# Operand sums of the seven-product stages placed anew, with the scale chain in two parts

## The chip, the cores and the metric

The kernel runs on one core of a Trainium2 chip. Its time is the device time of one execution in microseconds (us). The engines are named as in the profile: PE (TensorE, matmuls), PEld (its weight loads), DVE (VectorE), ACT (ScalarE), POOL (GpSimd) and SP (the engine that only issues DMAs). Each runs its own list of instructions in order, and waits on semaphores for the others.

## The reference

One transformer layer over x of 2048 x 1024. An attention part with 32 heads in four segments of 512 tokens, with a running memory matrix, makes `h = x + attention(layernorm(x)) @ wo`. A gated part follows:

```python
z  = gelu(layernorm(h) @ w_in)            # 2048 x 3584
z1 = z[:, :1792]
z2 = layernorm(z[:, 1792:])
g  = w_sp @ z2 + b_sp[:, None]            # w_sp is 2048 x 2048
h2 = h + (z1 * g) @ w_out                 # w_out is 1792 x 1024
```

The change touches the gated part alone.

## The kernel before

The attention part, which fills most of the first 340 us, is left as it is. Then these stages follow, and PE runs them in this order without a pause that is planned.

**The z2 half.** `z2_group(k, tc)` multiplies 128 tokens (tc, 16 of them) with 448 of the 1792 columns (k, 4 of them) in 8 matmuls; ACT applies the gelu, DVE takes the batch statistics (`z2_stats`), and with k = 3 also their aggregate, from which POOL makes the reciprocal deviation in two small instructions (tile `zrs`). Work for later stages is put between these groups: the list `aux`, filled by `at(q, f, ...)`, holds what is issued after group number q, where q is 16k + tc - 20. It holds the norms of `w_sp` and `w_in` for the scales, the half-precision copies of the z1 weights (`wz_half`), the first operand sums of the next stage (`hn_sum(0, ...)` on DVE, `sz_sum(0, ...)` on POOL).

**The z1 half.** z1 is made transposed. Blocks of 2 x 2 are multiplied with seven products in place of eight (Strassen's way in Winograd's form), which needs sums and differences of the operand blocks: `hn_sum(p, t, h)` for the activations (four sums t in two halves h, for each of the two token halves p) and `sz_sum(g, k)` for the weights (four for each of 14 steps g). `z1_step(g, k)` is product k of step g; the table `offs` orders the products, so that in steady state PE runs per step: 6 and 5, then 1 of the next step, 7, 2, 3 of the step before, and 4. Each is four matmuls of 512 columns. POOL makes the sums for step g + 1 when products 5 and 7 of step g are issued. What DVE and ACT do beside it is put into `todo1` by `on(g, k, f, ...)`, and is issued after product k of step g: the layer norm of z2 (`z2_apply`, after products 6 and 4), the second half's activation sums, the scale of `w_sp` (`scale_of`), its half-precision blocks (`sp_part`) and their sums (`sp_sum`).

**The gate, twice.** `gate(pr, ...)` multiplies half of `w_sp` with z2, again in seven products (b11, b12, b22, b21 and the sums t1 to t4), for seven column groups g. A product is `prod`: eight matmuls into one PSUM bank. Per group PE runs t2, t1, b11 of a later group (`p1`), t3, b21 of the next (`p2`), t4, b22. DVE takes the results from PSUM (`stt`), multiplies with z1 (`out`) and makes the sums of the z2 blocks (`ss`); POOL adds the bias (`tmp_s1b`), twice per group. The product t3 goes into the bank of t2, so it waits until DVE has read that bank.

**The output units between the gates.** 16 units of 14 matmuls each finish 1024 of the tokens. Each loads its piece of h (`fin_load`), adds on DVE, and stores. Both DMAs are issued by ACT, in ACT's program order: the load of unit n + 2, the store of unit n, and then, for n from 1 to 8, the square sum of an eighth of `w_out` (`wo_norm(n - 1)`, a 1792-element activation). In the same stretch SP loads the second half of `w_sp` by 16 transposing DMAs and, behind them in its queue, the two rows of biases (`brow_load(1)`); DVE converts and sums the blocks (`sp_half`, `sp_sum`). Two chains of scales run there. `scale_y` needs the square sums of the biases (`brow_sq`, on ACT) and of z1; it goes PE (`total`), DVE, POOL (four small instructions, the last a power), DVE, and scales the biases on ACT. `scale_w` needs the eight square sums of `w_out`, which POOL copies to `SQB`; a matmul (`total(8)`) sums them over the partitions. That matmul stands in PE's list after unit 11.

**The last stage.** The other 1024 tokens are multiplied with `w_out` in seven products too. Its weights and sums are made during the second gate (`ob_scale` on ACT, `ob_sum` on DVE, from the table in `each1`), its operand sums by `y_sum`. The last seventh of each sum (chunk 6) needs the gate's last result. `o_adds` makes three sums of a product and the residual on POOL; they are the operands of DVE's `o_stt`.

What orders each engine's work is thus the order in which the program issues it; no planner moves anything. Line numbers in the profile are all those of the recorder (L210), so groups are told by their tiles.

Of the kernel before, what the change touches and what calls it, by code (L numbers as in the profile page):

```python
# [10 lines left out]
ALU = mybir.AluOpType  # L11
# [247 lines left out]
def bass_sequential_preLN__memory_aug_infini_attn__mixer_gmlp__prompt_kernel(  # L259
# [17 lines left out]
    pe, act, dve, pool, sp = R.pe, R.act, R.dve, R.pool, R.sp  # L277
# [661 lines left out]
    def scale_of(k, n, b):  # L939
        b = next_bank() if b is None else b  # L940
        pe.matmul(PS[:, b, 0:n], ONES[:], SQB[:, 0:n], start=True, stop=True)
        dve.tensor_reduce(out=TOT[:], in_=PS[:, b, 0:n], axis=mybir.AxisListType.X, op=ALU.add)
        dve.tensor_single_scalar(TOT[:], TOT[:], 1e-30, ALU.max)
        if k:
            dve.reciprocal(TOP[:], TOT[:])
        else:
            pool.tensor_tensor(TOP[:], TOT[:], MHZ[:], ALU.pow)
        dve.tensor_single_scalar(TOP[:].bitcast(I32), TOP[:].bitcast(I32), 0x7F800000, ALU.bitwise_and)
        dve.tensor_single_scalar(SC[k][:], TOP[:], 8192.0, ALU.mult)
        dve.reciprocal(INV[k][:], SC[k][:])  # L950
# [40 lines left out]
    def at(q, f, *a):  # L991
        aux.setdefault(q, []).append((f, a))
# [12 lines left out]
    at(19, wz_norm, 3, 1)  # L1005
    at(20, pool.tensor_copy, SQB[:, 0:14], SQZ[:])
    at(25, scale_of, 1, 14, None)
    for k in range(8):
        at(26 + k, wz_half, k // 2, k % 2)
    for k in (1, 2, 3, 4):  # L1010
        at(35 + k, sz_sum, 0, k)

# [68 lines left out]
    def gate(pr, seam=lambda: None, mid=lambda: None, each=lambda g, k: None):  # L1081
        inv, zo = (INV[0], Z1T) if pr == 0 else (INVY, Z1X)
        t1, t2 = slice(1024 * pr, 1024 * pr + 512), slice(1024 * pr + 512, 1024 * pr + 1024)
        s1, s1b1, s1b2, u2, u3 = (TMP[k][:] for k in ("s1", "s1b1", "s1b2", "u2", "u3"))

        def stt(o, b, add):
            dve.scalar_tensor_tensor(o, bank(b), inv[:], add, ALU.mult, ALU.add)

        def out(v, g, i, t):
            dve.tensor_tensor(zo[:, g + 7 * i, t], v, Z1T[:, g + 7 * i, t], ALU.mult)  # L1090

        def ss(k, g):
            if g < 7:
                s_sum(k, g)

        def p1(g):
            prod(g % 3, a_blk(0, 0, g), "b11", True)

        def copy1(g):
            act.activation(s1, bank(g % 3), ACTF.Copy, scale=inv[:])  # L1100

        def p2(g):
            prod(g % 3, a_blk(0, 1, g), "b21", False)

        def c11(g):
            stt(u3, g % 3, BROW[0][:])
            out(u3, g, 0, t1)

        p1(0)
        copy1(0)  # L1110
        pool.tensor_tensor(s1b2, s1, BROW[1][:], ALU.add)
        pool.tensor_tensor(s1b1, s1, BROW[0][:], ALU.add)
        p1(1)
        p1(2)
        seam()
        p2(0)
        c11(0)
        for g in range(7):
            bb, bc = 3 + g % 2, 5 + g % 2
            prod(bb, SS[:, 1], "t2", True)  # L1120
            prod(bc, SS[:, 0], "t1", True)
            stt(u2, bb, s1b2)
            if g == 0:
                mid()
            ss(4, g)
            if g:
                ss(1, g + 1)
                ss(2, g + 1)
            if 1 <= g <= 3:
                p1(g + 2)  # L1130
            each(g, 0)
            prod(bb, SS[:, 2], "t3", False)
            if g < 5:
                copy1(g + 1)
                p2(g + 1)
            elif g == 5:
                p1(6)
                copy1(6)
            else:
                p2(6)  # L1140
            each(g, 1)
            stt(u3, bb, s1b2)
            stt(u3, bc, u3)
            out(u3, g, 1, t2)
            if not g:
                ss(1, 1)
                ss(2, 1)
            if g < 6:
                pool.tensor_tensor(s1b2, s1, BROW[1][:], ALU.add)
            ss(3, g + 1)  # L1150
            if g != 5:
                c11(min(g + 1, 6))
            prod(bb, a_blk(1, 1, g), "t4", False)
            each(g, 2)
            stt(s1b1, bb, s1b1)
            out(s1b1, g, 1, t1)
            if g < 6:
                pool.tensor_tensor(s1b1, s1, BROW[0][:], ALU.add)
            prod(bc, SS[:, 3], "b22", False)
            stt(u2, bc, u2)  # L1160
            out(u2, g, 0, t2)
            each(g, 3)
# [70 lines left out]
    def on(g, k, f, *a):  # L1233
        todo1.setdefault((g, k), []).append((f, a))

    for g in range(8):
        on(g, 6, lambda: zq and z2_apply())
        on(g, 4, lambda: zq and z2_apply(True))
    for k in range(8):
        on((0, 1, 2, 3, 4, 4, 5, 5)[k], 3 if k < 5 else (7, 3, 7)[k - 5], hn_sum, 1, (1, 2, 3, 4)[k // 2], k % 2)  # L1240
    on(1, 7, scale_of, 0, 16, None)
    for k, g, r in (("b11", 6, 3), ("b12", 6, 3), ("b22", 8, 3), ("b21", 12, 3)):
        for j in range(4):
            on(g, r, sp_load, 0, k, j)
# [1 line left out]
        for r in range(4):  # L1246
            on(g, (6, 7, 2, 4)[r], sp_part, k, r)
    for r in range(4):
        on(10 + r // 2, (3, 6, 3, 6)[r], sp_sum, "t1", r)
        on(12 + r // 2, (3, 6, 3, 6)[r], sp_sum, "t3", r)  # L1250
        on(13, (5, 7, 2, 4)[r], sp_sum, "t2", r)
    on(7, 3, brow_load, 0)

    offs = {1: -5, 6: 0, 5: 1, 7: 3, 2: 4, 4: 6, 3: 12}
# [69 lines left out]
    for n, u in enumerate(units):  # L1324
        if n + 2 < 16:
            fin_load(units[n + 2], act)
        out_unit(u, (lambda i: WO0[i // 7][:, i % 7, :]) if u[1] == 0 else
                 (lambda i: WO1[i // 7][:, i % 7, :]), act)
        if 1 <= n <= 8:
            wo_norm(n - 1)  # L1330
        if n == 1:
            sp_half("b11")
        if n == 4:
            sp_half("b12")
            sp_sum("t1")
        if n == 6:
            sp_half("b22")
            sp_sum("t3")
        if n == 8:
            sp_sum("t2")  # L1340
        if n == 9:
            brow_sq()
            scale_y()
            pool.tensor_copy(SQB[:, 0:8], SQY[:, 0:8])
        if n == 10:
            sp_half("b21")
            sp_sum("t4")
        if n == 11:
            scale_w()
        if n == 13:  # L1350
            for k in range(1, 4):
                s_sum(k, 0)
# [30 lines left out]
    def y_sum(k, g, lo=0, hi=7):  # L1383
        y = SY[g % 2]
        o = y[:, k - 1, lo:hi, :]
        a, b, op = {1: (y_blk(1, 0, g, lo, hi), y_blk(1, 1, g, lo, hi), ALU.add),
                    2: (y[:, 0, lo:hi, :], y_blk(0, 0, g, lo, hi), ALU.subtract),
                    3: (y_blk(0, 0, g, lo, hi), y_blk(1, 0, g, lo, hi), ALU.subtract),
                    4: (y_blk(0, 1, g, lo, hi), y[:, 1, lo:hi, :], ALU.subtract)}[k]
        if lo:  # L1390
            dve.scalar_tensor_tensor(o, a, 1.0, b, ALU.mult, op)
        else:
            dve.tensor_tensor(o, a, b, op)

    def fin_in(g):
        for i in range(2):
# [7 lines left out]
    def each1(g, k):  # L1404
        jobs = {(0, 0): [(ob_scale, "b11", 0)], (0, 1): [(ob_scale, "b11", 1)], (0, 2): [(ob_scale, "b12", 0)],
                (0, 3): [(ob_scale, "b12", 1)], (1, 0): [(ob_scale, "b22", 0)], (1, 1): [(ob_scale, "b22", 1)],
                (1, 2): [(ob_scale, "b21", 0)], (1, 3): [(ob_scale, "b21", 1)], (6, 0): [(fin_in, 0), (fin_in, 1)]}
        for n, (o, h) in enumerate([(o, h) for o in ("t1", "t2", "t3") for h in (0, 2, 4, 6)]):
            jobs.setdefault((1 + n // 2, (0, 3)[n % 2]), []).append((ob_sum, o, h))
        for f, *a in jobs.get((g, k), ()):  # L1410
            f(*a)
        if (g, k) == (6, 2):
            for x in range(1, 4):
                y_sum(x, 0, 0, 6)
# [16 lines left out]
    def o_s(k, g):  # L1431
        return lambda c: SY[g % 2][:, k - 1, c, :]
# [20 lines left out]
    fin_in(2)  # L1453
    fin_in(3)
    o_p1(0)
    o_adds(0)
    for x in range(1, 4):
        y_sum(x, 0, 6, 7)
    o_prod(3, o_s(2, 0), "t2", True, cs=range(6))
    o_p2(0)  # L1460
    o_c11(0)
    for g in range(4):
        bb, bc = 3 + g % 2, 5 + g % 2
        last = ((bc, 0, 512),) if g < 3 else ((bc, 0, 384), (7, 384, 512))
        f1, f12, f22, f21 = OT4[g % 2]
        if g == 0:
            o_prod(bc, o_s(1, g), "t1", True, cs=range(6))
        cs = range(6, 7) if g == 0 else range(7)
        o_prod(bb, o_s(2, g), "t2", True, cs=cs)
        for b, lo, hi in last:  # L1470
            o_prod(b, o_s(1, g), "t1", True, lo, hi, cs)
        o_stt(f12[:], bb, f12[:])
        if g == 0:
            ob_sum("t4", 0)
            ob_sum("t4", 2)
            ob_sum("t4", 4)
            ob_sum("t4", 6)
        y_sum(4, g)
        o_prod(bb, o_s(3, g), "t3", False)
        if g < 3:  # L1480
# [54 lines left out]
```

## Time and profile before

| what | us |
|---|---|
| median of 8 executions | 765.17 |
| lowest and highest of them | 761.75 and 770.49 |
| the profiled execution | 763.99 |
| its span, first to last instruction | 762.2 |
| PE busy (modelled ends) | 749.9 |
| DVE busy | 576.4 |
| ACT busy | 423.0 |
| POOL busy | 294.7 |

The span is 1.8 us less than the execution's own time. [...]matmuls of 512 columns that follow each other without a wait start 216 ns apart, though each is shown as 379 ns. A pause of PE is therefore read from the starts, less 0.216 us.

### The profile page before, as it was taken

How to read it: one execution, taken by the hardware profiler on the slowest of the kernel's cores; microseconds unless marked ns; L12 is line 12 of the kernel's file. 1: busy time of each engine (PE TensorE's matmuls, PEld its weight loads, DVE VectorE, ACT ScalarE, POOL GpSimd, SP SyncE). 2: the span in 40 equal slices, each digit the busy share in tenths (PEclk: the TensorE clock that was granted, in tenths of full speed). 3: DMA queues.
4: the chain of work that ended last, by engine and by line, in shares of the span. 5: the costliest groups of instructions: out<-in, count | busy, mean ns of one | idle time of the engine just before them, and what ended most of it. 6: DMA issues, size and time to landing. Idle time of an engine off the chain costs nothing.

```text
span 762.2 us, 13511 instructions
## 1 busy us (share of the span) xinstructions
PE 749.9 (98%) x5470; PEld 357.7 (47%) x5470; DVE 576.4 (76%) x1016; ACT 423.0 (56%) x519; POOL 294.7 (39%) x447
## 2 busy tenths in 40 slices
PE   8999999999999999999999999999999999999898
PEld 3445455555554445455554444444444444444344
DVE  5585589768974575759876986998884665999986
ACT  6777877787777768136984889623330525300000
POOL 2565456555654333000059987431130002212242
PEclk9999999999999999999999999999999999999999
DMA  9554556354425231778630036410039850001211
GB/s 300 168 162 85 89 80 143 88 84 93 104 57 125 84 71 43 199 198 251 194 112 1 0 69 112 96 57 1 0 56 175 229 183 8 0 1 56 63 49 56
DMA packets 136783, 75.09 MB, mean 99 GB/s; under 512 B 98064, under 2 KB 126480, under 8 KB 136720
## 3 DMA queue, kind: packets, MB, share of 16 engines
q1 hardware_dynamic: 129472, 67.40, 36.4%
q10 hardware_dynamic: 7248, 6.82, 3.1%
q8 instruction: 43, 0.70, 0.4%
q14 instruction: 20, 0.16, 0.1%
HBM read 42.74 MB, written 8.39 MB: 67 GB/s over the span
## 4 chain that ended last, share of the span: by engine, by line
PE 75%; DVE 11%; ACT 5%; issue 3%; DMA 3%; POOL 3%; ACTq 0%; DVEq 0%; POOLq 0%
PE ps L210 75%; ACT sj L210 3%; DVE tmp_u L210 2%; DMA sj<-in_B_w_sp_dram 2%; DVE z1x L210 2%; DVE ss L210 2%; ACT z L210 1%; DVE zt L210 1%; POOL sz L210 1%; POOL zrs L210 1%; DMA wv<-in_A_wv_dram 1%; DVE sy L210 1%; DVE fin L210 0%; DVE z1T L210 0%; ACT t4h L210 0%
## 5 line engine op out<-in xcount | busy, mean ns | idle before, releaser
L210 ACT ACTIVATE e<-ps 128x2048 bf16<-128x2048 f32 (+1 forms) x96 | 152.7, 1590 | 41.7 <-PE ps L210 41.4
L210 POOL TENSOR_SCALAR_AFFINE_SELECT e<-e 128x512 bf16<-128x512 bf16 x128 | 90.8, 722 | 132.1 <-ACT e L210 132.0
L210 PE MATMUL ps<-win,hnT 128*128 128x448 bf16 x512 | 98.4, 352 | 0.0
L210 POOL TENSOR_TENSOR tmp_s1b<-tmp_s,brow 128x512 f32<-128x512 f32 x28 | 33.9, 1214 | 131.8 <-DVE tmp_u L210 55.4
L210 PEld LDWEIGHTS ps<-win,hnT 128*128 128x128 bf16 x512 | 49.6, 98 | 46.3 <-issue 0.2
L210 PE MATMUL ps<-wv,xnT 128*128 128x512 bf16 x256 | 59.7, 380 | 1.4 <-DMA wv<-in_A_wv_dram 1.0
L210 PE MATMUL ps<-xnT,wk 128*128 128x512 bf16 x256 | 60.8, 380 | 0.0
L210 PE MATMUL ps<-xnT,wq 128*128 128x512 bf16 x256 | 60.5, 379 | 0.0
L210 DVE TENSOR_TENSOR zt<-ps,zt 128x512 f32<-128x512 f32 x70 | 47.5, 687 | 15.3 <-PE ps L210 12.7
L210 PE MATMUL ps<-wo,oT 128*128 128x512 bf16 x256 | 58.0, 379 | 0.0
L210 ACT ACTIVATE z<-ps 128x448 bf16<-128x448 f32 x60 | 30.7, 545 | 35.1 <-PE ps L210 35.0
L210 PE MATMUL ps<-w_out,z1T 128*128 128x512 bf16 x224 | 48.7, 379 | 0.0
L210 PEld LDWEIGHTS ps<-v,e 128*128 128x128 bf16 x1280 | 38.8, 96 | 14.0 <-issue 6.5
L210 DVE BATCH_NORM_STATS2 zst<-z 128x6 f32<-128x448 bf16 x64 | 37.9, 610 | 8.6 <-ACT z L210 8.4
L210 DVE RECIPROCAL rd<-ps 128x16 f32<-128x16 f32 x32 | 8.0, 250 | 47.0 <-PE ps L210 46.8
L210 PE MATMUL ps<-v,e 128*128 128x33 bf16 x1280 | 42.2, 178 | 0.0
L210 ACT ACTIVATE tmp_s<-ps,invy 128x512 f32<-128x512 f32 x7 | 4.8, 687 | 65.4 <-POOL tmp_s1b L210 36.9
L210 ACT ACTIVATE z1T<-zt,inv 128x512 bf16<-128x512 f32 x42 | 29.7, 718 | 16.1 <-DVE zt L210 16.0
L210 PEld LDWEIGHTS ps<-wo,oT 128*128 128x128 bf16 x256 | 24.1, 98 | 27.5
L210 PEld LDWEIGHTS ps<-xnT,wk 128*128 128x128 bf16 x256 | 22.6, 98 | 29.9 <-issue 5.0
L210 PEld LDWEIGHTS ps<-wv,xnT 128*128 128x128 bf16 x256 | 23.2, 98 | 28.3 <-DMA wv<-in_A_wv_dram 1.7
L210 POOL TENSOR_TENSOR sz<-wzh 128x512 f16<-128x512 f16 x28 | 33.2, 1186 | 8.2 <-PE ps L210 8.1
(206 smaller groups left out, 1484.8 us busy)
## 6 DMA issues: line engine op xcount, KB each, us to landing
sj<-in_B_w_sp_dram SPq DMA_DIRECT2D x16, 512.0 KB, 3.5
xch<-in_A_x_dram SPq DMA_DIRECT2D x16, 256.0 KB, 3.7
xr<-in_A_x_dram SPq DMA_DIRECT2D x16, 256.0 KB, 3.9
out_dram<-hch SPq DMA_DIRECT2D x16, 256.0 KB, 2.4
win<-in_B_w_in_dram SPq DMA_DIRECT2D x4, 896.0 KB, 5.3
wz<-in_B_w_in_dram SPq DMA_DIRECT2D x6, 512.0 KB, 7.6
wo<-in_A_wo_dram SPq DMA_DIRECT2D x1, 2048.0 KB, 8.4
fin<-out_dram ACTq DMA_DIRECT2D x16, 128.0 KB, 3.4
```

Source lines behind the costliest of these rows:

```text
L210: ins = getattr(e, op.name)(*op.args, **op.kw)
```

## The change

- `scale_of` is cut in two: the last three DVE instructions, which follow POOL's power, are a function of their own, `scale_end`. For the first scale it is called at once; for the second (`w_sp`) at product 2 of step 2, in place of product 7 of step 1.
- Four of the eight second-half activation sums (`hn_sum(1, 1 or 2, ...)`) move from the z1 half to the z2 half, after groups (3,1), (3,3), (3,5) and (3,7). The other four are issued after product 6 of steps 4 to 7, in place of after products 3 and 7 of steps 3 to 5.
- The `w_sp` sums t1 and t3 move from after product 3 to after products 5 and 6 of the same or an earlier point.
- In the second gate the first b11 product of group 2 goes behind t1 of group 0.
- Between the gates, `brow_sq` moves from unit 9 to unit 3, and `scale_y` from unit 9 to unit 4. The copy of the square sums to `SQB` stays at unit 9.
- In the second gate the sums `ob_sum` t1 to t3 are all issued at the first point of a group, up to three together, and the four of t4 join them from group 5 on. They were in the last stage.
- In the last stage the chunk-6 sums of `y_sum` run on POOL, ahead of `o_adds(0)`, in place of DVE behind it; and t1 of group 0 is issued whole behind the last chunk of t2, where its first six matmuls had been ahead of it.

```diff
@@ scale_of
             pool.tensor_tensor(TOP[:], TOT[:], MHZ[:], ALU.pow)
+
+    def scale_end(k):
         dve.tensor_single_scalar(TOP[:].bitcast(I32), TOP[:].bitcast(I32), 0x7F800000, ALU.bitwise_and)
         dve.tensor_single_scalar(SC[k][:], TOP[:], 8192.0, ALU.mult)
         dve.reciprocal(INV[k][:], SC[k][:])
@@ z2 half
     at(25, scale_of, 1, 14, None)
+    at(25, scale_end, 1)
     for k in range(8):
         at(26 + k, wz_half, k // 2, k % 2)
+    for k in range(4):
+        at(29 + 2 * k, hn_sum, 1, 1 + k // 2, k % 2)
@@ gate
         p1(1)
-        p1(2)
+        if not pr:
+            p1(2)
...
-            if 1 <= g <= 3:
+            if 1 - pr <= g <= 3:
                 p1(g + 2)
@@ z1 half
-    for k in range(8):
-        on((0, 1, 2, 3, 4, 4, 5, 5)[k], 3 if k < 5 else (7, 3, 7)[k - 5], hn_sum, 1, (1, 2, 3, 4)[k // 2], k % 2)
+    for k in range(4, 8):
+        on(*((4, 6), (5, 6), (6, 6), (7, 6))[k - 4], hn_sum, 1, (1, 2, 3, 4)[k // 2], k % 2)
     on(1, 7, scale_of, 0, 16, None)
+    on(2, 2, scale_end, 0)
...
-        on(10 + r // 2, (3, 6, 3, 6)[r], sp_sum, "t1", r)
-        on(12 + r // 2, (3, 6, 3, 6)[r], sp_sum, "t3", r)
-        on(13, (5, 7, 2, 4)[r], sp_sum, "t2", r)
+        on(*((10, 6), (10, 5), (11, 6), (11, 5))[r], sp_sum, "t1", r)
+        on(*((12, 5), (12, 6), (13, 3), (13, 6))[r], sp_sum, "t3", r)
+        on(*((13, 5), (13, 7), (13, 2), (13, 4))[r], sp_sum, "t2", r)
@@ output units
         if 1 <= n <= 8:
             wo_norm(n - 1)
+        if n == 3:
+            brow_sq()
+        if n == 4:
+            scale_y()
+        if n == 9:
+            pool.tensor_copy(SQB[:, 0:8], SQY[:, 0:8])
...
-        if n == 9:
-            brow_sq()
-            scale_y()
-            pool.tensor_copy(SQB[:, 0:8], SQY[:, 0:8])
@@ y_sum
-        if lo:
-            dve.scalar_tensor_tensor(o, a, 1.0, b, ALU.mult, op)
-        else:
-            dve.tensor_tensor(o, a, b, op)
+        (pool if lo else dve).tensor_tensor(o, a, b, op)
@@ each1
-        for n, (o, h) in enumerate([(o, h) for o in ("t1", "t2", "t3") for h in (0, 2, 4, 6)]):
-            jobs.setdefault((1 + n // 2, (0, 3)[n % 2]), []).append((ob_sum, o, h))
+        for n, (o, h) in enumerate([(o, h) for o in ("t1", "t2", "t3", "t4") for h in (0, 2, 4, 6)]):
+            jobs.setdefault(((1, 1, 1, 2, 2, 2, 3, 3, 3, 4, 4, 5, 5, 6, 6, 6)[n], 0), []).append((ob_sum, o, h))
@@ last stage
-    o_adds(0)
     for x in range(1, 4):
         y_sum(x, 0, 6, 7)
+    o_adds(0)
...
-        if g == 0:
-            o_prod(bc, o_s(1, g), "t1", True, cs=range(6))
-        cs = range(6, 7) if g == 0 else range(7)
-        o_prod(bb, o_s(2, g), "t2", True, cs=cs)
+        o_prod(bb, o_s(2, g), "t2", True, cs=range(7) if g else range(6, 7))
         for b, lo, hi in last:
-            o_prod(b, o_s(1, g), "t1", True, lo, hi, cs)
+            o_prod(b, o_s(1, g), "t1", True, lo, hi)
         o_stt(f12[:], bb, f12[:])
-        if g == 0:
-            ob_sum("t4", 0)
-            ob_sum("t4", 2)
-            ob_sum("t4", 4)
-            ob_sum("t4", 6)
```

## The prediction, made before the result was known

> **What bounds the kernel now.** I read the page's head first, then the list of what PE waited for, then the timelines around each pause.
>
> ```profile
> span 762.2 us, 13511 instructions
> ...
> PE 749.9 (98%) x5470; PEld 357.7 (47%) x5470; DVE 576.4 (76%) x1016; ACT 423.0 (56%) x519; POOL 294.7 (39%) x447
> ```
>
> PE is the bound, and the change takes no matmul away, so it can only give back pauses. The waits of PE (us in total, times, longest) show nearly all of them:
>
> ```profile
> PE ps L210 <- DVE zt L210: 1.7, 3, 0.8
> PE ps L210 <- POOL sqb L210: 1.7, 1, 1.7
> ...
> PE ps L210 <- DVE tmp_u L210: 1.2, 3, 0.6
> PE ps L210 <- DVE sy L210: 1.0, 1, 1.0
> ...
> PE ps L210 <- DVE ot L210: 0.9, 1, 0.9
> ```
>
> These ends are modelled. From the starts, less the 0.216 us pitch, I find from 400 us on: z1 half 0.80 (at 421.1), 0.44 (439.7), 0.94 (488.2); first gate 0.27 (515.2) and twice 0.1; scale matmul 1.84 (615.8); second gate 0.59, 0.76, 0.32 (685 to 707); last stage 1.16, 1.08, 0.30, 0.23 (721 to 732). Sum 9.0 us: no version of this change can gain more.
>
> The largest single one is the 1.84. Here are the timelines of ACT, then SP, then POOL around it (start us, duration us, engine, instruction, in brackets the idle time before it and what ended it):
>
> ```profile
> 597.29 1.70 ACT L210 ACTIVATE t4h<-w_out 128x1792 f16<-128x1792 bf16 x1
> ...
> 599.48 1.70 ACT L210 ACTIVATE t4h<-w_out 128x1792 f16<-128x1792 bf16 x1 [0.40 <-ACT t4h L210]
> ...
> 603.01 0.35 ACTq L210 DMA_DIRECT2D out_dram<-fin  x1
> ...
> 609.95 1.70 ACT L210 ACTIVATE t4h<-w_out 128x1792 f16<-128x1792 bf16 x1
> ...
> 612.63 0.63 ACT L210 ACTIVATE t4h<-brow 128x512 f16<-128x512 bf16 x1 [0.89 <-ACT t4h L210]
> ```
> ```profile
> 598.68 1.00 SPq L210 DMA_DIRECT2D brow<-in_B_b_sp_dram  x2
> ```
> ```profile
> 614.18 0.46 POOL L210 TENSOR_TENSOR tw<-tw,bsq 128x1 f32<-128x1 f32 x2 [42.98 <-ACT t4h L210]
> ...
> 615.52 0.19 POOL L210 CAST sqb<-sqy 128x8 bf16<-128x8 f32 x1
> ```
>
> The reader should see three things: the last of the eight square sums is done at 611.7; `SQB` is copied only at 615.5, because POOL stands before it in `scale_y`, waiting for the bias squares that ACT starts at 612.6; and the biases are issued by SP only at 598.7. They land 3.8 to 4.2 us after issue, by the answer for tile brow.
>
> [...]ACT's store at 603.01 waits for DVE's add, and the activation behind it (603.46) sat idle 2.19 us though its operands were there. [...]chunk sums of 128 elements on DVE took 1.24 and 1.12 us beside POOL's `ot` adds, and 0.28 once POOL was done. [...]512 elements take 1.16 us on POOL.
>
> **The change part by part.**
>
> *(a) Four activation sums into the z2 half.* A sum like them takes 0.68 us, 0.60 from start to start. DVE has no gap above 0.21 us from 384.7 to 393.5, so they add up: at the first row statistics of the groups (3,1), (3,2), ... the aggregates come 0.60, 0.48, 1.05, 1.05, 1.65, 1.65 and 1.69 us later (waits for ACT give 0.7 back in all). From the seventh on, POOL's chain carries it (POOL's timeline):
>
> ```profile
> 394.52 0.22 POOL L210 TENSOR_SCALAR zrs<-zmv 128x1 f32<-128x1 f32 x1 [0.29 <-DVE zmv L210]
> ...
> 395.36 1.16 POOL L210 TENSOR_TENSOR sz<-wzh 128x512 f16<-128x512 f16 x1
> ...
> 408.46 1.38 POOL L210 TENSOR_TENSOR sz<-wzh 128x512 f16<-128x512 f16 x1
> 409.91 1.16 POOL L210 TENSOR_TENSOR sz<-sz,wzh 128x512 f16<-128x512 f16 x1
> ```
>
> Between 395.36 and 411 POOL never pauses for more than 0.16 us (its own chain), so a start 1.7 later at 394.5 is 1.7 later at 409.91. That last sum (ends 411.07) is the operand of product 6 of step 1, which PE starts at 411.61: 0.54 of cover. PE stands 1.7 - 0.5 = 1.2 us. Bounds: 0, if DVE finds gaps that I don't see; 1.7. I take +1.2.
>
> *(b) Fewer sums and no power wait in the z1 half.* At 421.1 DVE reached the sum that PE waits for late by 1.14 us (wait for POOL's power), about 0.45 (three scale instructions) and 0.60 (one activation sum), more than the 0.80. All three leave that spot. At 439.7 two activation sums, 1.26 and 1.04 us beside POOL's, had stood before it; one stays, behind product 6 and with about 1.7 us until PE needs the next sum. -1.2 (0 to -1.2).
>
> *(c) The w_sp sums.* Two t1 sums of 1.39 and 1.47 us (beside POOL) at 479.4 and 485.5 become two of 0.6 in idle DVE time at 470 and 476. PE's wait at 488.2 falls from 0.94 to about 0.1, and DVE enters the first gate about 0.5 us earlier against PE than now, which covers the 0.27. -1.1 (0 to -1.2).
>
> *(d) `brow_sq` at unit 3, `scale_y` at unit 4.* The instructions are the same; what is queued behind them decides. ACT is through unit 3's square sum at 599.1 and now stands at `brow_sq` until the biases land, 598.7 + 4 = 602.7 and 603.1; done at 604.3. Behind it on ACT wait the load of unit 6, the store of unit 4 and five square sums. DVE, meanwhile, is at `scale_y` from 598.9 and stands until POOL's power: 604.3 plus the 2.0 us that this piece of chain takes now (bias squares 614.11, DVE's end 616.13) is 606.3. Behind it on DVE wait 1.28 + 2.29 us of `w_sp` work (`sp_half`, `sp_sum` of unit 4) and only then the add of unit 5, at 609.9; it is at 602.3 now. The store of unit 5 stands before the next square sum in ACT's list. So from there: store 610.5; square sum 4 at 611.0 to 612.9; store 6 at 611.5, sum 5 to 614.9; load 9 needs the buffer of store 5, which lands about 616.5 (stores issued at 608.6 and 612.0 took 6.8 and 5.4 us beside SP's 1.8 MB weight load, 608 to 618, which stays where it is); store 7 at 616.9; sum 6 to 619.2; load 10; store 8; sum 7 from 619.2 to 621.1. `SQB` follows at 621.3, and PE, ready at 613.9, waits 7.3 us where it waited 1.84. Were the DMAs as quick as outside that load (2 to 3 us), sum 7 would end at 619.9 and the wait be 6.1. If ACT were not held at all, the square sums would end at 611.7 and the wait vanish. +5.4 (from -1.8 to +6.5). No bank is short: with `total(28)` taken at unit 4, unit 12 reuses unit 5's bank, free at 610.6.
>
> *(e) Second gate.* DVE's list for a group, start to start: six stt 4.5, four out 3.1 (two beside POOL), four sums 2.5: 10.2 us, PE 56 x 0.216 = 12.1. Three weight sums at 0.60 make 12.0 in groups 1 to 3. In group 1 they end at 653.6, the read of t3's bank at 654.4, and t4, due 653.8, waits 0.65. In exchange DVE is no longer behind at group 4's t3 (0.59 gone), 0.3 arises at its t4, 0.6 at group 5's t3 as now, and group 6's 0.32 goes. Net -0.1 (-1.5 to +3). The moved b11 product fills time in which t3 of group 0 isn't late: 0.
>
> *(f) Last stage.* The timeline of before there:
>
> ```profile
> 716.61 0.69 DVE L210 TENSOR_TENSOR z1x<-tmp_u,z1T 128x512 f16<-128x512 f32 x1
> 716.67 4.09 POOL L210 TENSOR_TENSOR ot<-ot,fin 128x512 f32<-128x512 f32 x3 [11.26 <-ACT ot L210]
> ...
> 718.52 1.24 DVE L210 SCALAR_TENSOR_TENSOR sy<-z1x 128x128 f16<-128x128 f16 x1
> ...
> 719.79 1.12 DVE L210 SCALAR_TENSOR_TENSOR sy<-sy,z1x 128x128 f16<-128x128 f16 x1
> ...
> 722.49 0.82 PE L210 MATMUL ps<-z1x,sy 128*128 128x512 f16 x3 [0.92 <-DVE ot L210]
> ```
>
> A 128-element sum on POOL isn't in this trace; rows of 132 take 0.48 to 0.51, of 66 0.30, so I estimate 0.48. From 717.35 two of them end at 718.4, in time for PE at 718.5. The third, then the first `ot` add, end at 720.1; t1 whole keeps PE until 720.2; DVE's read of t2's bank needs that add and ends at 720.9, so t3 starts at 721.0, not 722.49. t4, now held by four weight sums on DVE (2.14 us), follows without its 0.30, and 0.2 of the last wait goes. -2.0 (-1.0 to -2.8).
>
> Sum: 1.2 - 1.2 - 1.1 + 5.4 - 0.1 - 2.0 = +2.2 us, on the profiled execution's 763.99 (span 762.2 and 1.8 around it): 766.2. The median of the runs is 1.2 above it, so I forecast 765.2 + 2.2 = 767.4.
>
> **The rivals.** *A: the change does what it says.* ACT isn't held at unit 3 and (d) is -1.8: sum -5.0, 760.2. For it: every operand but the biases is early. Against it: SP's issue at 598.7 stands behind 16 transposes that the change leaves alone. *B: VectorE bounds the second gate.* 12.0 of 12.1 us leaves 0.03 per weight sum; from a pitch above 0.63 on, groups 1 to 3 run late. At 0.9 (between 0.60 and the 1.38 of the one that met POOL) it is 0.8 a group and as much again in groups 4 to 6, about +3: 770.4, slower. Against it: the sums now in the gate keep 0.60. *C: the hold grows.* Each of the last three square sums stands behind a store and a load that need a landed DMA; 0.7 us more for each adds 2: 769.5. *D: the z2 half swallows the sums* and (a) is 0: 766.2, inside the forecast.
>
> **How the numbers follow.** Forecast with D 0.50, A 0.13, B 0.14, C 0.23. About 0.5% (3.8 us) is what a measurement of this kernel tells from no change. A is nearly all faster (0.11); the forecast's own range, 764 to 770, is nearly all within; B and about 0.20 of C, with 0.05 of the forecast's upper end, are slower. Faster 0.11, same 0.50, slower 0.39. The range runs from the near side of A, 761.5, to the far side of B and C, 772, leaving 0.1 on each side.
>
> **What would show it.** Right: the bias squares on ACT at about 602.8, DVE idle from 599 to 606 before `top`, the `sqb` copy near 621, and PE's wait on it 6 to 7 us, now the longest; a wait of PE for `sz` near 412; none at 421, 440 and 488; t3 of the last stage about 1.5 us nearer to the gate's end. Wrong: a `sqb` copy before 614 (rival A), or weight sums `z1x` and `z2h` of 0.9 us and more (B).

## The result and the profile after

The changed kernel takes 769.87 us (median of 19 executions, 768.52 to 771.32), the kernel before 764.59 (54 executions beside it). The ratio is 1.0058, with a 95% interval of 1.0040 to 1.0076 (the two medians alone give 1.0069): half a percent slower. The profiled execution took 769.02 us with a span of 767.3, so the span grew by 5.1 us. My forecast was 767.4, from a sum of +2.2.

The list of what PE waited for (us in total, times, longest), after:

```profile
PE ps L210 <- POOL sqb L210: 7.8, 1, 7.8
PE ps L210 <- DVE tmp_u L210: 1.5, 4, 0.6
...
PE ps L210 <- DVE zt L210: 0.6, 1, 0.6
PE ps L210 <- POOL sz L210: 0.6, 1, 0.6
PE ps L210 <- DVE ot L210: 0.4, 1, 0.4
```

Most of the waits that the change aimed at are shorter or gone (`zt`, `ot`; `sy` has left the list), but the one for `tmp_u`, in the second gate, went from 1.2 to 1.5, the one for `sz` is new, and the wait for `SQB` has grown to more than all others together. From PE's starts, as in the prediction (start to start, less 0.216 us), the pauses from 400 us on are:

| step | before | after | predicted | measured |
|---|---|---|---|---|
| (a) z2 half | 0.1 | 0.79 (409.6), 0.72 (413.0), 0.1 | +1.2 | +1.5 |
| (b) z1 half | 0.80, 0.44 | none | -1.2 | -1.2 |
| (c) w_sp sums | 0.94, 0.27 | 0.09 | -1.1 | -1.1 |
| (d) scale matmul | 1.84 | 8.00, and 1.59 in slow matmuls | +5.4 | +7.7 |
| (e) second gate | 0.59, 0.76, 0.32 | 0.65, 0.35, 0.32, 0.81, 0.06, 0.12 | -0.1 | +0.6 |
| (f) last stage | 1.16, 1.08, 0.30, 0.23 | 0.52 | -2.0 | -2.2 |
| sum | | | +2.2 | +5.3 |

Step (d) follows in the timelines of after: ACT, then DVE, POOL and PE (start, duration, instruction, in brackets the idle time before it and what ended it).

```profile
601.98 0.63 ACT L210 ACTIVATE t4h<-brow 128x512 f16<-128x512 bf16 x1 [3.44 <-DMA brow<-in_B_b_sp_dram]
...
609.74 0.35 ACTq L210 DMA_DIRECT2D out_dram<-fin  x1
610.20 1.70 ACT L210 ACTIVATE t4h<-w_out 128x1792 f16<-128x1792 bf16 x1 [3.54 <-DVE fin L210]
...
616.03 1.70 ACT L210 ACTIVATE t4h<-w_out 128x1792 f16<-128x1792 bf16 x1 [2.22 <-DMA out_dram<-fin]
...
617.85 1.70 ACT L210 ACTIVATE t4h<-w_out 128x1792 f16<-128x1792 bf16 x1
```
```profile
604.94 0.15 DVE L210 TENSOR_SCALAR top<-top 128x1 int32<-128x1 int32 x1 [6.43 <-POOL top L210]
...
605.50 1.29 DVE L210 TENSOR_SCALAR b12h<-b12r,sc 128x4096 f16<-128x4096 bf16 x1
606.82 2.29 DVE L210 TENSOR_TENSOR t1h<-b12h,b11h 128x4096 f16<-128x4096 f16 x1
609.03 1.28 DVE L210 TENSOR_TENSOR fin<-fin,ps 128x512 bf16<-128x512 bf16 x2
```
```profile
619.71 1.08 POOL L210 CAST sqb<-sqy 128x8 bf16<-128x8 f32 x1 [14.79 <-ACT t4h L210]
```
```profile
607.66 5.34 PE L210 MATMUL ps<-w_out,z1T 128*128 128x512 bf16 x24
620.84 0.19 PE L210 MATMUL ps<-sqb,ones 128*128 128x8 bf16 x1 [7.83 <-POOL sqb L210]
620.88 5.43 PE L210 MATMUL ps<-w_out,z1T 128*128 128x512 bf16 x17
```

ACT stands 3.44 us for the biases, DVE 6.43 us for the power that needs their squares; behind that DVE has two pieces of `w_sp` work before the add of unit 5 (609.03), and the late add holds ACT for another 3.54 us in front of the store at 609.74; and the last square sum starts at 617.85, where before the eighth had ended at 611.7. The last line shows the surprise: 17 matmuls take 5.43 us, and 24 took 5.34. The first eight of the 17 start about 427 ns apart (up to 624.20), the others 216. The view by stretches (width, busy us of PE, PEld, DVE, ACT and POOL with counts, PE clock, DMA share, GB/s) says why:

```profile
614.00:616.00 2.00, 0.00 (x0) 0.00 (x0) 0.99 (x2) 0.00 (x0) 0.00 (x0) 1.00 0.49 170
616.00:618.00 2.00, 0.00 (x0) 0.00 (x0) 2.00 (x2) 1.94 (x3) 0.00 (x0) 0.83 0.64 173
618.00:620.00 2.00, 0.00 (x0) 0.00 (x0) 2.00 (x4) 1.64 (x2) 0.29 (x1) 0.50 0.54 179
...
622.00:624.00 2.00, 2.00 (x6) 0.76 (x5) 1.89 (x4) 0.00 (x0) 0.00 (x0) 0.50 0.18 63
624.00:626.00 2.00, 2.00 (x11) 0.85 (x9) 0.86 (x5) 0.00 (x0) 0.55 (x1) 0.96 0.41 131
```

While PE stood still its granted clock fell to 0.50 (at 617.3 us, since the slice from 616 has a mean of 0.83), and it came back to 1.00 only at 624.1 (0.96 in the slice from 624). That is where the starts go from 427 to 216 ns apart; of the times, more below.

### The profile page after: what moved, and what is told of

The parts are those of the page before. It is cut to its first block, busy times and chain, and to the rows that moved or that the text cites. A ratio compares the mean times of both kernels' runs of the same rounds, so it can differ in the third digit from the quotient of the medians.

```text
span 767.3 us, 13511 instructions
## 1 busy us (share of the span) xinstructions
PE 751.2 (98%) x5470; PEld 358.8 (47%) x5470; DVE 573.0 (75%) x1013; ACT 421.6 (55%) x519; POOL 294.9 (38%) x450
## 4 chain that ended last, share of the span: by engine, by line
PE 78%; DVE 12%; DMA 3%; ACT 3%; issue 2%; POOL 2%; ACTq 0%; DVEq 0%; POOLq 0%
PE ps L210 78%; DVE z1x L210 3%; DVE tmp_u L210 3%; ACT sj L210 2%; DVE ss L210 2%; DMA sj<-in_B_w_sp_dram 2%; POOL zrs L210 1%; DMA wv<-in_A_wv_dram 1%; ACT z L210 1%; DVE zst L210 1%; DMA fin<-out_dram 1%; DVE tmp_s1b L210 1%; POOL sz L210 0%; DVE wzh L210 0%; DVE zmv L210 0%
## 5 line engine op out<-in xcount | busy, mean ns | idle before, releaser
L210 PE MATMUL ps<-w_out,z1T 128*128 128x512 bf16 x224 | 50.3, 387 | 0.0
```

What stands on the lines that cost most here:

```text
L210: ins = getattr(e, op.name)(*op.args, **op.kw)
```

## The experiments

**Theory H**: `scale_y`, issued early, stands in DVE's and POOL's lists until the biases' squares exist; what is queued behind it makes the column sums late. **Rivals**: *S*, the extra time is spread over the other parts of the change; *C*, the stores and loads of the output tiles make it, whatever ACT does; *A*, holding ACT at unit 3 is enough by itself (C and A here are not the prediction's). For the slow matmuls: *K*, PE's clock; *M*, something in the memory at that moment.

**1. The scale chain back at unit 9, everything else as changed.**

```diff
-        if n == 3:
-            brow_sq()
-        if n == 4:
-            scale_y()
         if n == 9:
+            brow_sq()
+            scale_y()
             pool.tensor_copy(SQB[:, 0:8], SQY[:, 0:8])
```

> The changed kernel with the bias squares, the scale chain and the copy back at unit 9. Theory H (the hold): PE's 8.0 us wait for the copied square sums, and the 1.5 us of slow matmuls behind it, give way to the old wait of about 1.8, so 7.7 us less than the changed kernel: 762 us, 0.997 of the kernel before. Rival S (the loss is spread over the stages, from sums that meet GpSimd or crowd VectorE): the wait at units 3 to 11 is made good elsewhere, and 766 us or more remain.

Measured: 761.35 us, ratio 0.9960 (0.9937 to 0.9983). The pause is 1.42 us, no matmul is slow. S falls: without (d) the rest of the change is a gain, and at full clock (a mean granted clock of 1.000) a clear one (12 of the 20 executions, median 760.85; of the kernel before 30 of 59, 763.00).

**2. The scale chain early, in the kernel before.** The reverse: `brow_sq` at unit 3 and `scale_y` at unit 4, alone.

```diff
+        if n == 3:
+            brow_sq()
+        if n == 4:
+            scale_y()
         if n == 9:
-            brow_sq()
-            scale_y()
             pool.tensor_copy(SQB[:, 0:8], SQY[:, 0:8])
```

> The kernel before with the bias squares at unit 3 and the scale chain at unit 4, nothing else. H: the wait of 1.84 becomes 8.0, and 8 or 9 matmuls behind it start 0.43 us apart: 7.7 us more, 772 us, 1.010. S: less than 4 us more, since the other parts carry a share of the loss.

Measured: 772.92 us, ratio 1.0089 (1.0051 to 1.0127); pause 7.92 us, then 14 slow matmuls. Step (d) alone costs more than the whole change does.

**3. The biases earlier.** SP issues them ahead of the last eight transposes.

```diff
     for k in ("b11", "b12", "b22", "b21"):
+        if k == "b22":
+            brow_load(1)
         for j in range(4):
             sp_load(1, k, j)
-    brow_load(1)
```

> The changed kernel with SP's load of the two bias rows ahead of the transposes of b22 and b21. H: the biases land near 582, ACT is not held at unit 3 and VectorE 3.4 us in place of 6.4 at unit 4; the chain of stores and square sums still runs through the weight load, so a wait of 2 to 3 us is left and no slow matmuls behind it: about 7 us less than the changed kernel, 763 us. Rival C (congestion: loads and stores beside the 1.8 MB weight load make the square sums late, whenever the biases land): the wait stays above 5 us.

Measured: 763.90 us, ratio 0.9987 (0.9962 to 1.0012). ACT's timeline:

```profile
595.97 1.70 ACT L210 ACTIVATE t4h<-w_out 128x1792 f16<-128x1792 bf16 x1
...
597.79 0.63 ACT L210 ACTIVATE t4h<-brow 128x512 f16<-128x512 bf16 x1
```

The squares follow their forerunner without a wait, the copy comes at 614.4, and the pause is 2.49 us without a slow matmul behind it. C, which wanted more than 5 us, falls; the late landing of the biases is what starts the long pause. DVE still waits 3.35 us for the power in this run.

**4. ACT held, but nothing queued on the scale of Y.** `brow_sq` stays at unit 3; `scale_y` goes behind the copy, which gets columns 28 to 35 of a wider `SQB` (the lines for the wider tile and for the offset in `total` are not shown).

```diff
-        if n == 4:
-            scale_y()
         if n == 9:
-            pool.tensor_copy(SQB[:, 0:8], SQY[:, 0:8])
+            pool.tensor_copy(SQB[:, 28:36], SQY[:, 0:8])
+            scale_y()
```

> The changed kernel with the bias squares at unit 3 as there, but the scale chain at unit 9, behind the copy of the square sums, which has its own columns. ACT is held for the biases, VectorE is not. H: ACT's hold of 3.4 us is mostly caught up by unit 11, the copy is made near 614 and PE waits 1 to 2 us: 762 us. Were ACT's hold the whole cause, the wait would be 5 us or more and the time 767.

Measured: 768.67 us, ratio 1.0058 (1.0042 to 1.0074), and nothing decided. The copy was made at 612.05, as H has it, but the ones-matmul of `scale_y` at unit 9, which reads columns 0 to 27, waited for it:

```profile
612.05 0.19 POOL L210 CAST sqb<-sqy 128x8 bf16<-128x8 f32 x1 [42.49 <-ACT t4h L210]
```
```profile
612.30 0.20 PE L210 MATMUL ps<-sqb,ones 128*128 128x28 bf16 x1 [5.60 <-POOL sqb L210]
```

The two column ranges don't overlap, and yet the reader of one waited for the writer of the other. Run 5 puts 8 bytes more between them and the wait is gone; how near is too near isn't shown.

**5. The same with the copy 64 bytes from the first column** (columns 32 to 39).

> The changed kernel with the bias squares left at unit 3, so that ScalarE still waits there for the bias transfer, but the scale of Y (its ones-matmul, its GpSimd chain and the biases' scaling) issued at unit 9, behind the copy of the column sums, which gets SBUF columns of its own, 64 bytes from the others. Theory H (the copy is late because GpSimd's queue stands on the scale chain, which stands on the squares): ScalarE is still held until about 602, but makes up for it; the copy is done near 612, about when TensorE wants it, the pause ahead of the ones-matmul is under 0.7 us and no matmul after it is slow: 760.4 us, ratio 0.9945 (0.992 to 0.997). Rival A (holding ScalarE at unit 3 is by itself what delays the column sums): the pause stays at 5 us or more, 766 us or more, ratio 1.002 or above.

Measured: 760.80 us, ratio 0.9941 (0.9919 to 0.9963). ACT is still held, for 3.33 us until 600.65, yet the copy comes at 612.44 and PE doesn't stand at all:

```profile
607.72 5.77 PE L210 MATMUL ps<-w_out,z1T 128*128 128x512 bf16 x25
613.33 0.17 PE L210 MATMUL ps<-sqb,ones 128*128 128x8 bf16 x1
613.36 4.91 PE L210 MATMUL ps<-w_out,z1T 128*128 128x512 bf16 x22
```

A falls. ACT makes up for a hold of 3.4 us; what can't be made up is the hold that `scale_y` hands to DVE (6.43 us, then 3.6 us of `w_sp` work ahead of unit 5's add) and through the store back to ACT. That the copy stands in POOL's queue behind `scale_y`, as the expectation also has it, plays no part: in the changed kernel POOL was through its part of `scale_y` at 604.9, and then stood 14.79 us for ACT's last square sum.

**6. Work for PE in the pause.** 30 matmuls of 512 columns, whose result nobody reads, ahead of the ones-matmul.

```diff
     def total(n):
         b = next_bank()
+        if n == 8:
+            for i in range(30):
+                pe.matmul(PS[:, b, :], Z1T[:, i % 7, 0:128], WO1[0][:, i % 7, :], start=True, stop=True)
```

> The changed kernel with 30 matmuls of 512 columns, of operands already in SBUF and with a result that nobody reads, issued ahead of the ones-matmul of the last scale: 30 x 0.216 = 6.5 us of TensorE work inside its pause of 8.0 us. Nothing on any other engine changes. Theory K (the eight matmuls of 427 ns after the pause come from TensorE's clock, which drops when it stands still): the ones-matmul still waits for GpSimd's copy until about 620.8, but now for 1.5 us only, the matmuls after it start 216 ns apart again, and the kernel ends 1.5 us earlier than the changed kernel: 768.3 us, ratio 1.004 (1.002 to 1.006). Rival M (they are slow because of what the memory or the other engines do at that moment): they stay at 427 ns, and the time stays at 769.9, ratio 1.0058.

Measured: 766.13 us, ratio 1.0001 (0.9976 to 1.0026), and no pause is left. That is 2.2 us better than expected, so something else had changed too. The fillers read `z1T`, and SP's 1.8 MB load into it, issued at 607 in the changed kernel, moved behind the last of them, which ended at 618.6: the DMA share is 0.15 in the slice from 612 and 1.02 in that from 620, where the changed kernel has 1.03 and 0.61. The copy now came 16.55 us after the bias squares' start (600.51 to 617.06), where it had been 17.73 (601.98 to 619.71). The ratio hides a difference at full clock: 13 of the 14 executions here had it, of the 67 of the kernel before only 37, and these (median 763.77) are 2.3 us quicker than run 6.

**7. The same fillers without `z1T`** (the matrix of ones in its place).

```diff
-                pe.matmul(PS[:, b, :], Z1T[:, i % 7, 0:128], WO1[0][:, i % 7, :], start=True, stop=True)
+                pe.matmul(PS[:, b, :], ONES[:], WO1[0][:, i % 7, :], start=True, stop=True)
```

> The changed kernel with 30 matmuls of 512 columns in TensorE's pause ahead of the ones-matmul, now of the matrix of ones and a half of w_out, so that no reader of z1T is added and the load into z1T starts near 607 as in the changed kernel. Theory K (TensorE's clock drops while it stands still): the copy is as late as in the changed kernel (near 620), the pause that is left is about 1.5 us, the matmuls after it start 216 ns apart: 1.55 us less than the changed kernel, 768.3 us, ratio 1.0038 (1.002 to 1.006). Rival M (transfers or other engines make those matmuls slow): 427 ns stay, 769.9 us, ratio 1.0058. If the load into z1T was not what made the first filled kernel better than expected, it comes out at 1.000 again.

Measured: 767.19 us, ratio 1.0046 (1.0030 to 1.0061); granted clock 1.000 in all five executions, where the changed kernel's 19 had 0.996 (12 of them) or 0.993 (7). PE's timeline:

```profile
612.85 6.64 PE L210 MATMUL ps<-w_out,ones 128*128 128x512 bf16 x30
620.43 0.18 PE L210 MATMUL ps<-sqb,ones 128*128 128x8 bf16 x1 [0.94 <-POOL sqb L210]
620.47 5.77 PE L210 MATMUL ps<-w_out,z1T 128*128 128x512 bf16 x26
```

The ones-matmul is as late as before, but the 26 behind it start 216 ns apart. K holds in the trace, M falls. By ratio the two kernels' intervals overlap; but every execution of this one (766.88 to 768.10) is under every one of the changed kernel (768.52 to 771.32). The medians lie 2.7 us apart, where the expectation had 1.6.

**8. The load into `z1T` later**, from ACT's queue at unit 12.

```diff
+        if n == 12:
+            act.dma_start(Z1T[:, :, 0:512], wout[:, :, 512:D])
...
-    sp.dma_start(Z1T[:, :, 0:512], wout[:, :, 512:D])
```

> The changed kernel with the load into z1T (the second half of w_out, on SyncE's queue from 607) issued from ScalarE's queue at unit 12, so near 623. Theory L (that load shares the DMA engines with the stores and loads of the output tiles at 609.7 to 615, which land 5.1 to 5.4 us after their issue there and 2.1 before it): those land in about 2.1 us again, the waits of ScalarE (2.2 us for a store) and VectorE (1.0 us for a load) before the last column sums shrink, the copy comes about 1.2 us earlier, the pause is 6.6 to 7 us and still followed by slow matmuls: 768.6 us, ratio 1.0042 (1.002 to 1.006). Rival N (the chain behind the bias squares sets it alone): pause 8.0, ratio 1.0058.

Measured: 769.45 us, ratio 1.0064 (1.0045 to 1.0083): no gain in time. Its trace does what L says: the store of unit 5 (610.68) has landed 2.3 us after its issue at the latest, since the load into its buffer is issued at 612.96 (5.4 in the changed kernel), ACT's wait of 2.22 us for a store has become one of 1.05 for DVE's add, DVE's of 1.00 is gone, and the copy comes 16.55 us after the squares' start, 1.18 sooner. But the pause is still 7.3 us, and in this execution the squares started 0.9 later and the slow stretch held 13 matmuls (2.6 us) and not 8 (1.59). So the load is a part of the lateness, of 1.2 us; that it is worth anything in time isn't shown.

**9. The four activation sums back in the z1 half** (steps 0 to 3, product 3).

```diff
-    for k in range(4):
-        at(29 + 2 * k, hn_sum, 1, 1 + k // 2, k % 2)
...
+    for k in range(4):
+        on(k, 3, hn_sum, 1, (1, 2, 3, 4)[k // 2], k % 2)
```

> The changed kernel with the two moved pairs of operand sums put back into the z1 half (stages 0 to 3, product 3). Theory H: the pauses near 409.6 and 413.0 (1.5 us together in the changed kernel) go, and that near 421 doesn't come back or comes back under 0.3, since only two of the four stages' other jobs stand there: 768.4 us, ratio 1.004 (1.002 to 1.006). Rival: VectorE is full there too, the pause near 421 comes back with 0.8 and that near 440 with 0.4, and the placement is worth nothing: 769.6, ratio 1.0055.

Measured: 769.58 us, ratio 1.0048 (1.0028 to 1.0068): the rival's answer, at another place. The z1 half now has pauses of 0.12, 0.52 and 0.65 at 433.5, 436.6 and 443.3, since sums there are long beside POOL's (DVE's timeline):

```profile
434.34 1.64 DVE L210 TENSOR_TENSOR ht<-hnT 128x1024 f16<-128x1024 bf16 x1
...
441.05 1.64 DVE L210 TENSOR_TENSOR ht<-hnT 128x1024 f16<-128x1024 bf16 x1
```

And the pauses at 409.2 and 412.6 were there (0.92 and 0.72) although no sum stands in the z2 half any more. In this execution ACT had waited there for a block of `w_sp`:

```profile
392.52 1.91 ACT L210 ACTIVATE sj<-sj 128x2048 bf16<-128x2048 bf16 x1 [0.72 <-DMA sj<-in_B_w_sp_dram]
```

Put in order, the fourteen profiles of this study say: with neither the sums nor this wait 0.2 us or less at those two places (three kernels), with the wait alone 1.6 (this one), with the sums alone 1.0 to 2.2 (seven), with both 2.3 to 2.8 (three). As far as this sorting goes, the delay is that of the chain of row statistics, and the sums are one of two things that cause it; ACT's wait was never varied by itself.

**10. The weight sums of the second gate placed anew**: mostly after product 2, which stands behind t3 in a group.

```diff
-            jobs.setdefault(((1, 1, 1, 2, 2, 2, 3, 3, 3, 4, 4, 5, 5, 6, 6, 6)[n], 0), []).append((ob_sum, o, h))
+            jobs.setdefault(((1, 0), (1, 2), (1, 2), (1, 2), (2, 0), (2, 2), (2, 2), (2, 2), (3, 0), (4, 0), (5, 0), (5, 3), (6, 0), (6, 0), (6, 0), (6, 2))[n], []).append((ob_sum, o, h))
```

> The changed kernel with the 16 jobs of operand sums of the second gate placed anew: after product 2 of the stages where the old ones ran VectorE full, and none behind another in stage 5. Theory H (each pause of the second gate is VectorE being behind with the stage's own work by what the jobs ahead of it take): of the six pauses, 2.3 us together, about 0.7 go, with the same wait for GpSimd's copy: 769.2 us, ratio 1.0048 (1.003 to 1.007). Rival (the pauses are set by the release of the banks, whatever the jobs do): 2.3 us stay, ratio 1.0058.

Measured: 769.80 us, ratio 1.0077 (1.0061 to 1.0093), over the range expected. The gate's pauses fell from 2.30 to 1.61 us (0.08, 0.36, 0.55, 0.55, 0.07), as H has it; but the last stage's rose from 0.52 to 1.11 (0.19, 0.30, 0.61), because a weight sum (0.34 from start to start) now stands ahead of the operand sums there, and PE, 0.4 us earlier, meets results that come no sooner. Given back in part, and no gain in time; the pause ahead of the ones-matmul was 8.45 us here.

**11. The last stage's part alone, in the kernel before.** The `y_sum`, `o_adds` and t1 edits, with the t4 weight sums left where they were.

```diff
-        if lo:
-            dve.scalar_tensor_tensor(o, a, 1.0, b, ALU.mult, op)
-        else:
-            dve.tensor_tensor(o, a, b, op)
+        (pool if lo else dve).tensor_tensor(o, a, b, op)
...
-    o_adds(0)
     for x in range(1, 4):
         y_sum(x, 0, 6, 7)
+    o_adds(0)
...
-        if g == 0:
-            o_prod(bc, o_s(1, g), "t1", True, cs=range(6))
-        cs = range(6, 7) if g == 0 else range(7)
-        o_prod(bb, o_s(2, g), "t2", True, cs=cs)
+        o_prod(bb, o_s(2, g), "t2", True, cs=range(7) if g else range(6, 7))
         for b, lo, hi in last:
-            o_prod(b, o_s(1, g), "t1", True, lo, hi, cs)
+            o_prod(b, o_s(1, g), "t1", True, lo, hi)
```

> The kernel before with the last stage's part of the change alone: the last chunk of the three sums of Y on GpSimd, ahead of the chain of output adds, and the product t1 whole. Theory H: the pauses near 721 and 722.5 (1.16 and 1.08 us) and the ones after them (0.30 and 0.23) become a single one of 0.5 to 0.8: 762.5 us, ratio 0.9972 (0.9955 to 0.999). Rival: GpSimd's three sums in a row (0.42 to 0.48 us each) are later than VectorE's were, the pause only changes its place: ratio 1.000.

Measured: 763.68 us, ratio 0.9977 (0.9955 to 1.0000); but the last stage's pauses are 0.59, 1.47 and 0.77, 2.83 together against 2.77 before. The gain in the profile lies elsewhere (0.53 us at the ones-matmul, 1.84 before), and at full clock there is next to none in time: 763.53 us (20 of 22 executions) against 763.77 (37 of 67). DVE and PE show where it went:

```profile
719.55 0.75 DVE L210 SCALAR_TENSOR_TENSOR ot<-ps,invo,ot 128x512 f32<-128x512 f32 x1 [0.56 <-POOL ot L210]
720.22 3.39 DVE L210 TENSOR_TENSOR z2h<-w_out0h,z1x 128x1024 f16<-128x1024 f16 x4
...
724.07 0.74 DVE L210 SCALAR_TENSOR_TENSOR ot<-ps,invo,ot 128x512 f32<-128x512 f32 x1
```
```profile
724.87 1.68 PE L210 MATMUL ps<-z2h,z1x 128*128 128x512 f16 x7 [1.31 <-DVE ot L210]
```

The four t4 sums, 3.39 us beside POOL's adds, stand between two reads of PSUM that PE needs. The gain of (f) thus needs both edits, as far as the runs go: the chunk sums on POOL and the t4 sums moved into the gate, where they are among the sums that cost the 0.6 of (e). The move of the t4 sums alone was not run.

**12. Runs 5 and 10 together.**

> Two edits of the changed kernel together: the scale of Y issued behind the column sums' copy in columns of its own (760.8 us alone) and the sums of the second gate placed as in the run before. If both effects add: 760.1 us, ratio 0.9936 (0.992 to 0.996), under both kernels. If the second gate's placement is worth nothing: 760.8, ratio 0.9945.

Measured: 760.04 us, ratio 0.9952 (0.9936 to 0.9968), against 764.04 for the kernel before beside it. It beats both kernels; run 5 alone does too, and the two can't be told apart.

## Why the prediction was right, and where it was not

The changed kernel came out slower, inside the range, by the mechanism that I named. Bias squares on ACT: 601.98, predicted 602.8. DVE idle before `top` until 604.94, predicted 606. Store of unit 5: 609.74, predicted 610.5. The four square sums behind it start at 610.20 and end at 619.55, predicted 611.0 to 621.1. Copy done: 620.8, predicted near 621. PE waits for `sz` at 413.0, predicted near 412, and none at 421 and 440. Runs 1, 2, 3 and 5 show the chain. The likeliest case was still "within 0.5%", and the ratio is 1.0058: the sum was 3.1 us short. The measured time is at the upper edge of the forecast's own range (764 to 770) and nearest to rival C's 769.5, though most of what was missing is in no rival; the number alone would not have told them apart.

*Step (d), the pause.* I set the copy against PE's arrival in the kernel before, 613.9, and took the gains of (a) to (c), -1.1, beside it. But a copy that waits for SP's biases doesn't come sooner because PE does. PE was there at 612.85, and waited 8.0, not 7.3, although the copy was 0.5 earlier than predicted. Read at the ones-matmul itself (615.77 before, 620.84 after), everything up to it cost 5.1 us; my terms gave 4.3.

*Step (d), what follows the pause.* The eight slow matmuls, 1.59 us, are in no term. I read the pause as time lost once, and had not reckoned with matmuls behind it that start 427 ns apart. This is the largest miss; run 7 takes it away.

*Step (e).* Predicted -0.1, measured +0.6. Group 1's t4 waits 0.65, as said. Group 4's t3 keeps 0.35 and group 6's 0.12, where I had both gone, and group 5's rose to 0.81. I had let DVE catch up fully in the groups with two sums; it doesn't. Run 10 shows that the placing of the sums is worth 0.7 of the 2.3 us; rival B didn't happen, since the sums did not slow down: the three of group 1 take 1.89 us together.

*Steps (a), (b), (c), (f).* (a): POOL's chain came 1.87 us later where I said 1.7, and PE's stand came in two parts, the first of which I had not named. At 409.61 PE waits for DVE's read of a bank (`zt`), which stands behind the late row statistics on DVE (408.93, before 407.47); at 413.02 it waits for `sz`. The total is still set by `sz`, as said, since the first wait only takes from the second (POOL's timeline, then PE's):

```profile
396.39 0.22 POOL L210 TENSOR_SCALAR zrs<-zmv 128x1 f32<-128x1 f32 x1 [0.21 <-DVE zmv L210]
...
411.82 1.15 POOL L210 TENSOR_TENSOR sz<-sz,wzh 128x512 f16<-128x512 f16 x1
```
```profile
409.61 1.04 PE L210 MATMUL ps<-z1x,sz 128*128 128x512 f16 x4 [0.63 <-DVE zt L210]
...
413.02 1.25 PE L210 MATMUL ps<-z1x,sz 128*128 128x512 f16 x5 [0.55 <-POOL sz L210]
```

(b) and (c) hold to 0.1 us. (f): the three sums on POOL take less than my estimate of 0.48:

```profile
724.77 0.42 POOL L210 TENSOR_TENSOR sy<-z1x 128x128 f16<-128x128 f16 x1 [11.54 <-DVE z1x L210]
725.27 0.43 POOL L210 TENSOR_TENSOR sy<-sy,z1x 128x128 f16<-128x128 f16 x1
725.66 0.43 POOL L210 TENSOR_TENSOR sy<-z1x 128x128 f16<-128x128 f16 x1
726.04 3.76 POOL L210 TENSOR_TENSOR ot<-ot,fin 128x512 f32<-128x512 f32 x3
```

How much slower POOL is than DVE changes with the size: a sum of 128 elements takes 0.43 us on POOL against 0.28 on DVE (at 720.84 before), one of 512 takes 1.15 (at 411.82) against 0.42 (at 720.16 in run 10). The size of (f) is right to 0.2, but I gave it to the wrong edit: run 11 shows that those edits alone gain nothing in the last stage.

*The prediction's rivals.* A, "ACT isn't held", is what run 5 nearly makes, without freeing ACT: 760.8, and A's price was 760.2. C, "the hold grows with each DMA", happened in part: one wait of 2.22 us, 1.2 us by run 8.

## What to carry to other kernels

Before a step is moved earlier, look up when its last operand arrives, and list what stands behind it on each engine that it touches; the engine that waits first (here ACT, 3.4 us) may recover, while the one at the chain's end (DVE, 6.4 us) holds up the first again. Work out a join in absolute times on both sides: what one side gains ahead of it doesn't move an operand that comes from elsewhere. And when PE is to stand for several microseconds, add the slow matmuls behind the pause to the bill (here 1.6 to 2.8 us behind pauses of 7.3 to 8.0).

## What the hardware showed unexpectedly

- Pauses of 5.8 us (run 4), 7.3 (run 8), 7.9 (run 2) and 8.0 (the changed kernel) were followed by matmuls that start 427 ns apart; those of 2.49 (run 3), 1.84 (before) and 1.10 (run 7) were not. In the changed kernel the clock fell 4.3 us after PE's last matmul ended (613.0 to 617.3), in run 8 already after 2.4 (613.5 to 615.8). It came back 3.3 us after PE's next start in the changed kernel (620.84 to 624.15), in run 8 after 5.4 (620.66 to 626.1). So the half clock lasted 6.83 us in the one and 10.2 in the other, and the slow matmuls cost 1.59 us and 2.6; in run 2 they cost 2.8. The profiled executions of runs 4, 9 and 10 have the changed kernel's mean granted clock, 0.996, that of run 2 has run 8's, 0.993. What decides between the two lengths isn't shown. Run 8, half clock from 615.8 to 626.1 (columns as above):

```profile
614.00:616.00 2.00, 0.00 (x0) 0.00 (x0) 2.00 (x4) 0.95 (x3) 0.00 (x0) 0.96 0.19 61
...
626.00:628.00 2.00, 2.00 (x10) 0.88 (x9) 0.69 (x1) 0.00 (x0) 0.00 (x0) 0.98 0.00 0
```

- Half the clock for 6.83 us in 767 is a mean of 0.996, for 10.2 a mean of 0.993: these are the means of the two groups of executions of the changed kernel (means of 769.4 and 770.7 us). The kernel before has such executions as well. Of the 67 beside runs 5, 6, 9 and 11, 37 had 1.000 (median 763.77), 13 had 0.997 or 0.998, and 17 had 0.996 or less (median 770.2). Its one trace has 1.000, so where PE stood in the others isn't known; a difference of a few us between two kernels can come from how many such executions each had.
- Stores and loads of output tiles, issued from 609.7 to 610.7 beside the 1.8 MB load, land 5.1 to 5.4 us after their issue; that load (issued at 607.0) takes 7.9 itself, and those issued behind its end, from 615.2 to 617.9, land after 2.2 to 2.7. In the kernel before, beside the same load (608.0, 9.8 us), it is 3.9 to 6.8 for those issued from 607.7 to 611.6. In run 7 the store issued at 608.22 holds ACT until 615.64, 7.4 us later; in run 8, with the load moved away, the one at 610.68 no more than 2.3.
- Run 6 is 1.1 us under run 7, and the traces show a pause of that size: in run 7 the copy comes 19.72 us after the squares' start (600.46 to 620.18), in run 6 16.55, so that run 7 keeps a pause of 1.10 us that run 6 hasn't. The load thus costs that chain 3.2 us in run 7 and 1.2 in the changed kernel; why its effect differs is open.
